# Fillers before the first scores, key maxima and block sums moved, two weight quarters moved, two weight differences on GpSimd

## The chip, the cores and the metric

One core of one Trainium2 chip runs the whole program. TensorE (PE) multiplies, VectorE (DVE), ScalarE (ACT) and GpSimd (POOL) work beside it, SyncE (SP) issues most of the transfers. The metric is the time of one execution on the device, in microseconds (us). A run of three executions before the change gave a median of 551.72 us.

## The reference

Three blocks follow each other. First comes attention for 2 batches, 8 heads and 768 positions of 64 values: every query sees the keys less than 16 positions away, and beside them one summary per block of 32 positions (the maximum of the keys, the mean of the values):

```
k_sum = k.reshape(B, H, nb, block, D).max(axis=3)
v_sum = v.reshape(B, H, nb, block, D).mean(axis=3)
scores_all = concat([where(|i-j| < 16, scale * q @ k.T, -1e9), scale * q @ k_sum.T + log(block)])
a = softmax(scores_all)
x = a @ concat([v, v_sum])
```

Then comes a mixture of eight experts over the 1536 tokens of 512 values. Each token goes to the expert with the largest logit, and is weighted with the softmax and a sigmoid gate:

```
e_idx = argmax(x @ w_gate)
out[t] = gate_w[t] * eom[t, e] * (relu(x[t] @ w1[e]) @ w2[e])
```

Last comes a gated projection, `(sigmoid(x @ w_gate) * (x @ w_val)) @ w_out`, with 1536 inner values.

## The kernel before

The large products are made of three products of parts: a value is split into a high part (written by ACT, `hi`) and the difference to it (`lo`, line 134, on DVE unless another engine is named), and high times high, high times low and low times high are summed in PSUM, the accumulators of TensorE.

**Attention** goes in 12 tiles of 128 queries (T = 0 to 5 the first batch, 6 to 11 the second). `s1` makes the scores of a tile in two halves: a mask (line 312), then four pairs of heads (line 316) against the keys and the key maxima, then a minimum of the (negated) scores on DVE (`nm`) and the exponentials on ACT. `s3` transposes the exponentials (line 344, copied as `aT` by ACT), `s4` multiplies them with the values (line 354), `s6` transposes the result to `xT` (line 370), `s7` makes the logits of the experts (line 379). The order over the tiles is written out in one loop over T; scores run ahead of the products by two tiles.

`ksum(b, p)` makes the maxima of the keys of batch b for the pair of heads p: five instructions on DVE, the last of which (line 255) writes them where `s1` reads them. `vsum_part` adds the values of blocks, for the second batch on GpSimd (lines 272 and 274). `place_sums(b)` transposes these sums with TensorE (line 286) and writes them into the value tiles `vt` (one half by DVE, the other by ACT at line 290, then copies on GpSimd at line 294). `keep_warm(n)` issues n matmuls whose result nobody uses (line 300, bf16, 128x512); eight of them run before the first mask. PSUM has banks by tags: A (3 banks), B (2), C (one tile of two banks, which also holds the result `xp` of `s4`) and M (1, for fillers, routing and single results).

**Experts.** `route` finds each token's expert and rank from the logits. `find_first` finds the tokens of the first item (an item is up to 256 tokens of one expert): `ff` is its generator, and `run(ff, n)` issues its next n stages. Its last stages are twelve small matmuls (line 608, which take `place`, written by DVE), two instructions on DVE and two gathers on GpSimd (line 613). `item_T` transposes the gathered tokens (line 642). `item_A(f)` is the f-th eighth of the first layer: twelve matmuls (line 653), then `hh` on ACT (line 655) and `hl` on DVE (line 656), which frees the bank of tag A. `item_B(f)` is the second layer. The weights are split by quarters: `split1(p)` for `w1`, `split2(p)` for `w2`, a high part by ACT and a difference by DVE (128x1024 each). There are seven items in the fixed part; the table of the items (`tb`, its tiles are named `o_...`) is worked out on DVE and GpSimd during the first and the second.

**The projection** follows, with its weights split in the same way (`wl` on GpSimd, `yb` on DVE).

Three sequences matter for the change: the first scores (lines 318 to 325), the loop over T (`ksum`, `place_sums` and `run(ff, 9)` stand at fixed T), and the stretch behind the loop (`item_A(0)`, `split1(1)`, `s6(11)`, `item_A(1)`, `run(p1, 1)`, `split1(2)`), with the loop over the items, where `split2(f // 2)` follows every even `item_A(f)`.

Of the kernel before, what the change touches and what calls it, by code (L numbers as in the profile page):

```python
# [10 lines left out]
F32 = mybir.dt.float32  # L11
# [22 lines left out]
C = 128  # L34
# [74 lines left out]
def moe_kernel(tc, A, out):  # L109
# [23 lines left out]
    def lo(o, i, h, eng=None):  # L133
        (eng or V).tensor_tensor(out=o, in0=i, in1=h.bitcast(F32), op=ALU.subtract)  # L134
# [145 lines left out]

    def place_sums(b):

        sp = ps.tile([128, 2, 512], F32, tag="C", bufs=1, name=f"sp{b}")[:, 0]
        for c in range(4):
            for p0 in (32, 96):
                PE.matmul(sp[p0:p0 + NB, c * 128:c * 128 + 128], vsum[b][:, c, 0:NB], ident, start=True, stop=True)
        heads = lambda x: x.rearrange("p (h x) -> p h x", h=H)
        first = vt[b, 0]
        ts(heads(first[32:32 + NB, 0, 1])[:, :, 0:D], heads(sp[32:32 + NB]), 1.0 / BLK, ALU.mult)
        SC.mul(heads(first[96:96 + NB, 0, 0])[:, :, 0:D], heads(sp[96:96 + NB]), 1.0 / BLK)  # L290
        for half in range(2):
            for par, p0 in ((0, 96), (1, 32)):
                n = 2 + half
                G.tensor_copy(vt[b, half][p0:p0 + NB, 3 - n:3, par], first[p0:p0 + NB, 0:1, par].to_broadcast([NB, n, VW]))

    def keep_warm(n):

        w = bank("M", 1)
        for _ in range(n):
            PE.matmul(w, warm[:, 0:128], warm, start=True, stop=True)  # L300

    def s1(T, halves=(0, 1)):

        b, m = divmod(T, TB)
        if ("a", T) not in st:
            st["a", T] = at.tile([128, 8, C], F32, tag="a", bufs=3, name=f"a{T}")
        a = st["a", T]
        sc = {half: bank("A", 3)[:, 0:4 * C].rearrange("p (g c) -> p g c", c=C) for half in halves}

        def mask(half):  # L310
            v = variant(2 * m + half)
            PE.matmul(sc[half], sel, mask4[:, v:v + 1].to_broadcast([67, 4, C]), start=True, stop=False)

        def score(half, pr):
            c0 = col_start(2 * m + half)
            PE.matmul(sc[half][:, pr], qz[T][:, pr, half], kg[b][:, pr, c0:c0 + C], start=False, stop=pr == 3)

        if T == 0:
            for half in halves:
                mask(half)  # L320
            for pr in range(4):
                for half in halves:
                    score(half, pr)
                if pr < 3:
                    keep_warm(4)
        for half in halves:
            if T:
                mask(half)
                for pr in range(4):
                    score(half, pr)  # L330
            scv = sc[half]
            nm = at.tile([128, 4], F32, tag="nm", bufs=4, name=f"nm{T}{half}")
            pace.append(red(nm, scv, ALU.min))
            for pr in range(4):
                SC.activation(out=a[:, half * 4 + pr], in_=scv[:, pr], func=AF.Exp, bias=nm[:, pr:pr + 1], scale=-1.0)
# [295 lines left out]
        hi(w1h[:, :, s], w1r[:, :, s])  # L631
        lo(w1l[:, :, s], w1r[:, :, s], w1h[:, :, s], eng)

    def split2(p):
        s = slice(2 * p, 2 * p + 2)
        hi(w2h[:, s], w2r[:, s])
        lo(w2l[:, s], w2r[:, s], w2h[:, s])

    def item_T(i, h, tag=("B", 2)):
        tp = bank(*tag).rearrange("p (g c) -> p g c", g=4)  # L640
        for c in range(4):
            PE.transpose(tp[:, c], xg[i % 2][:, h, c * 128:c * 128 + 128], ident)
        s = slice(h * 128, h * 128 + 128)
        hi(xTh[:, :, s], tp)
        lo(xTl[:, :, s], tp, xTh[:, :, s])
# [175 lines left out]
    def run(g, n=1):  # L821
        for _ in range(n):
            next(g, None)

    with tc.manual_schedule():
# [31 lines left out]
        for T in range(NT):  # L857
# [3 lines left out]
            if T < 2:  # L861
                for half in range(2):
                    s1(T + 1, (half,))
                    if T == 1 and half == 0:
                        place_sums(0)
                    s3(T, (half,))
                    if T == 0:
                        vsum_part(0, 2 + half)
                if T == 1:
                    spread_q(3)  # L870
            else:
                if T < NT - 1:
                    s3(T)
                if T == 3:
                    spread_q(5)
                if T == NT - 1:
                    item_T(0, 0, ("A", 3))
                    item_T(0, 1, ("A", 3))
                for t in q8:
                    s7(t)  # L880
                if T == NT - 2:
                    s3(T + 1)
                    split1(0)
                for t in now[:-1]:
                    s4(t)
                for t in first:
                    s1(t, (0,))
                if T == 8:
                    run(ff, 1)
                for t in q6:  # L890
                    s6(t)
                if T == 5:
                    place_sums(1)
                if 2 < T < NT - 3:
                    spread_q(T + 3)
                for t in first:
                    s1(t, (1,))
                if T == 2:
                    spread_q(4)
                if T == 3:  # L900
                    ksum(1, 1)
                if T == 8:
                    run(ff, 1)
                if T > 8:
                    run(g, 1)
            for t in now[-1:]:
                s4(t)
            if T == 8:
                run(ff, 9)
            for t in then:  # L910
                s1(t)
            for t in q7:
# [23 lines left out]
                    vsum_part(1, c)  # L936
            if T == 2:
                ksum(1, 0)
            if T == 3:
                ksum(1, 2)  # L940
                ksum(1, 3)
            if 2 < T < 7:
                load_q(T + 5)
            if T == 4:
                V.memset(low, 0.0)
                for e in range(1, 8):
                    V.memset(low[:, e, 0:e], 1.0)
# [34 lines left out]
        hl = mB.tile([128, 8, SLOT], F32R, name="hl")  # L982
        run(p1, 1)
        item_A(0)
        split1(1)
        s6(11)
        item_A(1)
        run(p1, 1)
        split1(2)
        item_gather(0, gidx[:, 16], S)  # L990
        item_gather(1, gidx[:, 17], S)
        item_A(2)
# [23 lines left out]
        for i in range(NSTAT):  # L1016
# [6 lines left out]
            if i:  # L1023
                for f in range(8):
                    item_A(f)
                    if f % 2 == 0:
                        split2(f // 2)
                    elif i > 1:
                        run(bg, 1)
                    if i == 1:  # L1030
                        if f in (1, 3, 4, 5):
                            run(tb, 1)
                        if f == 5:
                            for t in yrt:
                                G.memset(t, 0.0)
                            item_regs(2)
                            item_gather(2, gidx[:, 2])
# [221 lines left out]
```

## Time and profile before

| | |
|---|---|
| three executions | 551.72, 550.05, 551.89 us (median 551.72) |
| profiled execution | 552.54 us, of which its span is 550.7 us |
| PE busy | 535.8 us, 97% of the span |
| DVE, ACT, POOL busy | 388.1, 213.0 and 125.8 us (70, 39 and 23%) |

The span reaches from the first to the last record of the profile; 1.84 us of the execution lie outside it. Matmul ends are modelled, so that the rows below are best read by their starts. A row of the time line is: start, duration (of all its instructions, if it stands for several), engine, line, operation, result and operands, shape, number of instructions, and in brackets the idle time before it with what ended that.

### The profile page before, as it was taken

What the parts mean: (1) busy time and instruction counts of PE and PEld (TensorE: products, weight loads), DVE (VectorE), ACT (ScalarE), POOL (GpSimd) and SP (SyncE); (2) the same over time, 40 slices, a digit from 0 to 9 for tenths busy, and PEclk for the clock granted to TensorE, in tenths of its full rate; (3) what the DMA queues carried; (4) which work ended last, traced back from release to release, by engine and by line L of the source; (5) the groups of instructions that cost most, each with busy time, mean ns of one, the idle gap of its engine ahead of it and who ended that gap; (6) DMA issues with size and microseconds to landing.
All of it is one profiled execution on the core that took longest, in us unless ns stands there. A gap on an engine that the chain in (4) does not pass through costs nothing.

```text
span 550.7 us, 8924 instructions
## 1 busy us (share of the span) xinstructions
PE 535.8 (97%) x3236; PEld 456.5 (83%) x3236; DVE 388.1 (70%) x737; ACT 213.0 (39%) x390; POOL 125.8 (23%) x151
## 2 busy tenths in 40 slices
PE   8999989999999999999999999999999999999995
PEld 4788979888989989878888888888888888888884
DVE  4886768898778677853878899999998753323330
ACT  2786765755546455643221221211111442122110
POOL 3663145072101101000010111102101152212211
PEclk9999999999999999999999999999999999999998
DMA  8992368971568403216132323323322000001000
GB/s 326 411 412 88 132 231 273 335 277 39 183 244 280 160 6 119 70 57 211 39 114 78 114 80 112 115 83 109 114 76 77 1 2 38 20 38 39 21 37 39
DMA packets 31984, 71.63 MB, mean 130 GB/s; under 512 B 3056, under 2 KB 11712, under 8 KB 31936
## 3 DMA queue, kind: packets, MB, share of 16 engines
q1 hardware_dynamic: 28816, 60.96, 32.0%
q0 software_dynamic: 3120, 10.06, 5.5%
q8 instruction: 26, 0.43, 0.3%
q14 instruction: 22, 0.18, 0.1%
HBM read 72.53 MB, written 11.33 MB: 152 GB/s over the span
## 4 chain that ended last, share of the span: by engine, by line
PE 34%; issue 15%; POOL 5%; ACT 0%; POOLq 0%; DVE 0%; DVEq 0%; ACTq 0%
PE ps_A L1143 18%; PE ps_B L1143 15%; POOL out_dram L1191 3%; POOL yb L134 2%; PE ps_B L747 1%; POOLq L1255 0%; ACT yb L131 0%; ACT gs L131 0%; DVE gg L137 0%; POOLq L1191 0%; DVEq L137 0%; POOLq L134 0%; ACTq L131 0%
## 5 line engine op out<-in xcount | busy, mean ns | idle before, releaser
L1184 PE MATMUL ps_A<-yb,gs 128*128 128x512 f32 x432 | 98.1, 389 | 0.0
L1143 PE MATMUL ps_A<-yb,wh 128*128 128x512 f32 x312 | 96.8, 392 | 0.1
L1184 PEld LDWEIGHTS ps_A<-yb,gs 128*128 128x128 f32 x432 | 81.2, 188 | 16.8
L1143 PE MATMUL ps_B<-yb,wh 128*128 128x512 f32 x264 | 81.3, 390 | 0.0
L1143 PEld LDWEIGHTS ps_A<-yb,wh 128*128 128x128 f32 x312 | 57.9, 188 | 12.0 <-issue 0.6
L1143 PE MATMUL ps_A<-yb,wl 128*128 128x512 f32 x156 | 60.8, 390 | 0.0
L134 POOL TENSOR_TENSOR wl<-cvw,wh 128x512 fp32r<-128x512 f32 x20 | 26.7, 1334 | 137.7 <-ACT wh L131 137.7
L1143 PEld LDWEIGHTS ps_B<-yb,wh 128*128 128x128 f32 x264 | 49.6, 188 | 10.2
L1152 ACT ACTIVATE sg<-ps_A 128x512 f32<-128x512 f32 x36 | 21.4, 595 | 91.4 <-PE ps_A L1143 91.3
L653 PE MATMUL ps_A<-xTh,w1h 128*128 128x256 f32 x192 | 54.9, 286 | 1.0 <-DVE hl L656 1.0
L653 PE MATMUL ps_A<-xTh,w1l 128*128 128x256 f32 x192 | 54.5, 284 | 0.6 <-DVE w1l L134 0.6
L653 PE MATMUL ps_A<-xTl,w1h 128*128 128x256 f32 x192 | 54.4, 283 | 0.0
L1143 PE MATMUL ps_B<-yb,wl 128*128 128x512 f32 x132 | 51.4, 389 | 0.0
L131 ACT ACTIVATE gs<-gg 128x768 fp32r<-128x768 f32 x24 | 20.3, 846 | 69.6 <-PE ps_A L1184 67.4
L134 DVE TENSOR_TENSOR gs<-gg,gs 128x768 fp32r<-128x768 f32 x24 | 23.0, 958 | 34.2 <-ACT gs L131 34.1
L143 DVE TENSOR_SCALAR cva<-cva 128x512 f32<-128x512 f32 x72 | 43.3, 602 | 1.9
L134 DVE TENSOR_TENSOR w2l<-w2r,w2h 128x1024 fp32r<-128x1024 f32 x28 | 34.2, 1225 | 9.9 <-ACT w2h L131 9.1
L662 PE MATMUL yp<-w2h,hh 128*128 128x512 f32 x96 | 39.0, 407 | 0.0
L653 PEld LDWEIGHTS ps_A<-xTh,w1h 128*128 128x128 f32 x192 | 36.8, 192 | 1.6 <-DVE hl L656 1.4
L662 PE MATMUL yp<-w2h,hl 128*128 128x512 f32 x96 | 37.6, 392 | 0.0
L662 PE MATMUL yp<-w2l,hh 128*128 128x512 f32 x96 | 37.5, 391 | 0.0
L653 PEld LDWEIGHTS ps_A<-xTh,w1l 128*128 128x128 f32 x192 | 36.8, 192 | 0.8 <-DVE w1l L134 0.8
(232 smaller groups left out, 965.5 us busy)
## 6 DMA issues: line engine op xcount, KB each, us to landing
w1r<-in_w_dram SPq DMA_DIRECT2D x28, 512.0 KB
w2r<-in_w_dram SPq DMA_DIRECT2D x28, 512.0 KB
raw<-in_wgv_dram SPq DMA_DIRECT2D x24, 512.0 KB
vt<-in_vv_dram SPq DMA_DIRECT2D x12, 520.0 KB
raw<-in_wo_dram SPq DMA_DIRECT2D x12, 512.0 KB
kg<-in_kg_dram SPq DMA_DIRECT2D x8, 496.0 KB
y_c<-yt SPq DMA_DIRECT2D x13, 256.5 KB
yr<-y_c SPq DMA_DIRECT2D x12, 256.5 KB
```

What stands on the lines that cost most here:

```text
L131: SC.activation(out=o, in_=i, func=AF.Copy)
L134: (eng or V).tensor_tensor(out=o, in0=i, in1=h.bitcast(F32), op=ALU.subtract)
L143: V.tensor_scalar(out=o, in0=a, scalar1=s1, scalar2=s2, op0=op0, op1=op1)
L653: PE.matmul(hp, w[:, c, s], x[:, c], start=n == 0, stop=n == 11)
L662: PE.matmul(yp[h], x[:, f, s], w[:, f], start=f == 0 and n == 0, stop=f == 7 and n == 2)
L747: PE.transpose(tp[:, c], r[:, c * 128:c * 128 + 128], ident)
L1143: PE.matmul(pp, w[:, c], x[:, c], start=n == 0, stop=n == 11)
L1152: SC.activation(out=sg, in_=pp, func=AF.Sigmoid)
L1184: PE.matmul(po, g2[:, x, f % 6], yb[f // 4][w][:, f % 4], start=f == 0 and n == 0, stop=f == 11 and n == 2)
L1191: d = G.indirect_dma_start(out=out[:, :], out_offset=bass.IndirectOffsetOnAxis(ap=row_id[:, t:t + 1].bitcast(U32), axis=0), in_=ot, in_off ...
```

## The change

- In the first tile's scores, the fillers `keep_warm` stand before each of the four pairs of heads, 4, 3, 3 and 2 of them; before, 4 stood behind each of the first three pairs. Both make 12.
- `place_sums` takes the bank of tag M. Before, it took the tile of tag C.
- `ksum(1, 1)` moves from T = 3 to the end of T = 2, `ksum(1, 2)` from the end of T = 3 to the old place of `ksum(1, 1)`. `ksum(1, 3)` stays.
- `place_sums(1)` moves from the middle of T = 5 to the end of T = 4.
- `run(ff, 9)`, with the matmuls and the gathers of `find_first`, moves from the last third of T = 8 to T = 9, behind `s3(9)`.
- `split1(1)` moves from behind `item_A(0)` to T = 11, behind `item_T`; `split1(2)` from behind `run(p1, 1)` to the place ahead of it.
- `split2` takes an engine. For item 1, `split2(0)` and `split2(1)` make their differences on GpSimd.

```diff
     def place_sums(b):
-        sp = ps.tile([128, 2, 512], F32, tag="C", bufs=1, name=f"sp{b}")[:, 0]
+        sp = bank("M", 1)
...
         if T == 0:
             for half in halves:
                 mask(half)
-            for pr in range(4):
+            for pr, n in enumerate((4, 3, 3, 2)):
+                keep_warm(n)
                 for half in halves:
                     score(half, pr)
-                if pr < 3:
-                    keep_warm(4)
...
-    def split2(p):
+    def split2(p, eng=None):
         s = slice(2 * p, 2 * p + 2)
         hi(w2h[:, s], w2r[:, s])
-        lo(w2l[:, s], w2r[:, s], w2h[:, s])
+        lo(w2l[:, s], w2r[:, s], w2h[:, s], eng)
...
                 if T < NT - 1:
                     s3(T)
+                if T == 9:
+                    run(ff, 9)
...
                     item_T(0, 1, ("A", 3))
+                    split1(1)
...
-                if T == 5:
-                    place_sums(1)
...
                 if T == 3:
-                    ksum(1, 1)
+                    ksum(1, 2)
...
-            if T == 8:
-                run(ff, 9)
...
             if T == 2:
                 ksum(1, 0)
+                ksum(1, 1)
             if T == 3:
-                ksum(1, 2)
                 ksum(1, 3)
...
             if T == 4:
+                place_sums(1)
                 V.memset(low, 0.0)
...
         item_A(0)
-        split1(1)
         s6(11)
         item_A(1)
+        split1(2)
         run(p1, 1)
-        split1(2)
...
                     if f % 2 == 0:
-                        split2(f // 2)
+                        split2(f // 2, G if i == 1 and f < 4 else None)
```

On DVE, around the end of T = 2 (the `ks` and `kt` rows with line 255 behind them are one `ksum`, `nm` the minima of a half tile of scores, `xT` the copy behind `s6`). Before:

```order
L255 COPY kg_107<-ks_481 128x6x24
L146 TENSOR_REDUCE nm_510<-ps_A 128x4
L372 COPY xT_521<-ps_B 128x512
L146 TENSOR_REDUCE nm_531<-ps_A 128x4
L146 TENSOR_REDUCE ks_537<-kg_107 128x6x2
L146 TENSOR_REDUCE kt_538<-kg_107 128x12
L146 TENSOR_REDUCE ks_537<-kg_107 128x6
L137 TENSOR_TENSOR ks_537<-kt_538 128x6
L255 COPY kg_107<-ks_537 128x6x24
```

and after:

```order
L255 COPY kg_107<-ks_482 128x6x24
L146 TENSOR_REDUCE ks_489<-kg_107 128x6x2
L146 TENSOR_REDUCE kt_490<-kg_107 128x12
L146 TENSOR_REDUCE ks_489<-kg_107 128x6
L137 TENSOR_TENSOR ks_489<-kt_490 128x6
L255 COPY kg_107<-ks_489 128x6x24
L146 TENSOR_REDUCE nm_518<-ps_A 128x4
L371 COPY xT_529<-ps_B 128x512
L146 TENSOR_REDUCE nm_539<-ps_A 128x4
```

The second pair's maxima stand ahead of a tile's two minima where they stood behind them.

On POOL, in the second item (`o_es` belongs to the table of the items, `yt` to the output of the first item, `yr` are buffers of the projection). Before:

```order
L524 COPY o_es<-cs 128x8 x2
L707 COPY yt_1749<-xg_87 128x1
L707 COPY yt_1753<-xg_87 128x1
L1035 MEMSET yr_1639 128x520
L1035 MEMSET yr_1640 128x520
```

and after:

```order
L523 COPY o_es<-cs 128x8 x2
L706 COPY yt_1750<-xg_87 128x1
L706 COPY yt_1754<-xg_87 128x1
L134 TENSOR_TENSOR w2l<-w2r,w2h 128x1024 x2
L1033 MEMSET yr_1640 128x520
```

Two differences of 128x1024 stand between the output's copies and the buffers' memsets.

On DVE, in the first four eighths of the second item (`hl` ends an eighth, `o_le`, `o_lf` and `o_tf` are the table's). Before:

```order
L656 SCALAR_TENSOR_TENSOR hl<-ps_A,hh 128x256
L134 TENSOR_TENSOR w2l<-w2r,w2h 128x1024
L656 SCALAR_TENSOR_TENSOR hl<-ps_A,hh 128x256
L137 TENSOR_TENSOR o_le<-o_cc,ck 128x104 x2
L137 TENSOR_TENSOR o_le<-o_le 128x104
L137 TENSOR_TENSOR o_lf<-o_le,o_es 128x728
L656 SCALAR_TENSOR_TENSOR hl<-ps_A,hh 128x256
L134 TENSOR_TENSOR w2l<-w2r,w2h 128x1024
L656 SCALAR_TENSOR_TENSOR hl<-ps_A,hh 128x256
```

and after:

```order
L655 SCALAR_TENSOR_TENSOR hl<-ps_A,hh 128x256 x2
L137 TENSOR_TENSOR o_le<-o_cc,ck 128x104 x2
L137 TENSOR_TENSOR o_le<-o_le 128x104
L137 TENSOR_TENSOR o_lf<-o_le,o_es 128x728
L655 SCALAR_TENSOR_TENSOR hl<-ps_A,hh 128x256 x2
```

The two `w2l` are gone from DVE; the table's four instructions stand between the second and the third `hl` as before.

## Rows read from the trace of the kernel before

**Rows 1.** Time line of TensorE, the first scores.

```profile
7.03 1.20 PE L316 MATMUL ps_A<-kg,qz 128*128 128x128 f32 x4 [0.30 <-ACT qz L239]
8.02 1.92 PE L300 MATMUL ps_M<-w2r 128*128 128x512 bf16 x4
9.73 1.06 PE L316 MATMUL ps_A<-kg,qz 128*128 128x128 f32 x4
...
11.99 0.61 PE L316 MATMUL ps_A<-kg,qz 128*128 128x128 f32 x4
12.44 1.03 PE L300 MATMUL ps_M<-w2r 128*128 128x512 bf16 x4
13.30 0.61 PE L316 MATMUL ps_A<-kg,qz 128*128 128x128 f32 x4
```

**Rows 2.** Time line of DVE in the same stretch.

```profile
10.87 0.23 DVE L255 COPY kg<-ks 128x144 f32<-128x144 f32 x1
13.72 1.29 DVE L146 TENSOR_REDUCE nm<-ps_A 128x4 f32<-128x512 f32 x2 [2.62 <-PE ps_A L316]
```

**Rows 3.** Time line of all engines, keys and block sums of the second batch.

```profile
41.89 0.49 PE L316 MATMUL ps_A<-kg,qz 128*128 128x128 f32 x2 [0.79 <-DVE kg L255]
...
43.17 0.23 POOL L274 TENSOR_TENSOR vs<-w1r 128x24 f32<-128x24 f32 x1
...
48.84 1.06 PE L286 MATMUL sp<-ident,vs 128*24 128x128 f32 x16
...
51.42 1.16 PE L354 MATMUL xp<-vt,aT 128*64 128x65 f32 x32 [0.31 <-ACT vt L290]
```

**Rows 4.** Time line of TensorE and POOL, tokens of the first item and its first layer.

```profile
71.18 0.84 PE L608 MATMUL ps_M<-ckb,place 128*128 128x2 bf16 x9 [0.38 <-DVE place L143]
...
75.34 1.00 POOL L613 DMA_INDIRECT xg<-x_t,gix  x1 [0.31 <-issue]
...
83.53 1.09 PE L642 MATMUL ps_A<-ident,xg 128*128 128x128 f32 x8
...
92.25 0.39 PE L653 MATMUL ps_A<-xTh,w1l 128*128 128x256 f32 x1 [0.62 <-DVE w1l L134]
```

**Rows 5.** Time line of POOL, DVE and TensorE, first eighths of the second item.

```profile
118.81 1.34 POOL L707 COPY yt<-xg 128x1 int32<-128x1 int32 x2
...
120.36 0.43 DVE L137 TENSOR_TENSOR o_le<-o_cc,ck 128x104 f32<-128x104 f32 x2
...
120.83 0.27 DVE L137 TENSOR_TENSOR o_le<-o_le 128x104 f32<-128x104 f32 x1
...
121.19 0.92 DVE L137 TENSOR_TENSOR o_lf<-o_le,o_es 128x728 f32<-128x728 f32 x1
...
121.92 0.28 PE L653 MATMUL ps_A<-xTh,w1l 128*128 128x256 f32 x1
122.03 0.42 DVE L656 SCALAR_TENSOR_TENSOR hl<-ps_A,hh 128x256 fp32r<-128x256 f32 x1
...
122.50 0.39 PE L653 MATMUL ps_A<-xTh,w1h 128*128 128x256 f32 x1 [0.30 <-DVE hl L656]
```

**Rows 6.** Differences on GpSimd, a group of the page: total, mean ns, idle before.

```profile
L134 POOL TENSOR_TENSOR wl<-cvw,wh 128x512 fp32r<-128x512 f32 x20 | 26.7, 1334 | 137.7 <-ACT wh L131 137.7
```

**Rows 7.** Time line of DVE and POOL, differences on both engines.

```profile
438.21 2.38 DVE L134 TENSOR_TENSOR yb<-wo,yb 128x512 fp32r<-128x512 f32 x2
...
438.42 5.13 POOL L134 TENSOR_TENSOR yb<-wo,yb 128x512 fp32r<-128x512 f32 x3 [18.40 <-ACT yb L131]
...
441.72 0.68 DVE L134 TENSOR_TENSOR yb<-wo,yb 128x512 fp32r<-128x512 f32 x1
```

**Rows 8.** Stretches at the end: busy time of each engine, granted clock, DMA.

```profile
544.00:546.00 2.00, 0.36 (x2) 0.00 (x0) 0.46 (x1) 0.34 (x1) 0.49 (x1) 1.00 0.00 0
546.00:547.00 1.00, 0.00 (x0) 0.00 (x0) 0.00 (x0) 0.00 (x0) 0.48 (x1) 1.00 0.00 0
547.00:548.00 1.00, 0.00 (x0) 0.00 (x0) 0.00 (x0) 0.00 (x0) 0.00 (x0) 0.79 0.68 262
```

## The prediction, before the change was run

> **What bounds the kernel now.** I read the page first: TensorE is busy for 97% of the span (the table above), so that only its waits can be won, and its work at the slow rate. Then I went through TensorE's time line for starts that have an idle time in brackets. They add up to some 6 us, and nearly all stand before 126 us: from there until its last matmul, 0.36 into the stretch from 544 [rows 8], TensorE hardly waits (0.27 at 238 and 0.15 at 246), and the chain of work that ended last is its own matmuls. So what is won before 126 us moves the end by the same amount, and what is lost there does so too. Last I read, for each step that the change moves, the time line of the engine that releases TensorE there, and looked for other work of that engine in the new place.
>
> A term is the idle time of a row. The ends of matmuls are modelled, so such an idle time is short by a little: in the second item one product starts at 121.92 and the next at 122.50 [rows 5], 0.58 apart, while products of this kind follow each other by 0.12. That is a loss of 0.46 where the bracket says 0.30. I add 0.15 to each of the four waits that go and are read from a bracket, 0.6 in all.
>
> **The start.** Before, TensorE has a hole of 0.30 ahead of the first scores, which wait for `qz`. The first four fillers are spaced (9.73 - 8.02) / 4 = 0.43 apart, the last four (13.30 - 12.44) / 4 = 0.215 [rows 1]: these are the two levels of the clock, 1.2 and 2.4 GHz, and the rate rose a little before 11.99, some 11.7. The scores end at 13.7, when DVE's minima, idle for 2.62, begin [rows 2]. The change keeps the twelve fillers, and puts four of them where the hole is, and three ahead of the next pair. What it can give lies between two ends. If the rate rises at 11.7 as before, 0.3 of the hole is won and 0.1 in the order: 0.4. If it rises as the scores begin, the work left is 12 x 0.215 for fillers and 4 x 0.45 for pairs (12.44 - 11.99) [rows 1], 4.4 us from 6.7 on, or 11.1. But the fourth pair needs its maxima, which DVE ends at 10.87 + 0.23 = 11.10 [rows 2]. Its matmuls then end at 11.55, 2.2 before the old end. I take 2.1, since the row that the change touches is the hole, and behind the hole the rate rose while TensorE had no other; this is the weakest of my choices, and 0.4 stays as a rival.
>
> The Trainium skill ("TensorE: Matmul & The Clock Gate", Part 1) says that the moment at which the clock rises is not tied to the kernel's start and shifts from run to run, and advises against fitting to it. By that rule some executions would give 0.4 and some 2.2, and the median could lie anywhere between.
>
> **Key maxima.** `ksum(1, 1)` now stands before two minima of scores instead of behind them, so that its result, and that of `ksum(1, 2)`, are ready long before use. The wait of 0.79 at 41.89 [rows 3] goes. What is late next is the minima that stand behind it, and with them the exponentials on ACT. No row shows that; five small instructions take about as long as two minima, 1.3 [rows 2], and scores run two tiles ahead of their products. I take 0.1, within 0 and 0.7.
>
> **Block sums.** `place_sums(1)` leaves the place at 48.84 and goes to about 43 to 46. The wait of 0.31 for ACT's write into `vt` [rows 3] goes, since a whole step of scores then lies between. Does GpSimd deliver its last sum in time? It ends at 43.17 + 0.23 = 43.40 [rows 3], and TensorE, 3 us earlier here by the terms so far, reaches the sums at about 42.9 to 43.1. It first does three of the four columns (three quarters of 1.06, 0.8), so it reaches the last at 43.8: covered by 0.4. If that cover fails, it costs 0.4. The bank of tag M instead of C frees the tile of `xp`. ACT's write now stands ahead of a copy `aT` for the next tile: 0.1.
>
> **First tokens.** The wait of 0.38 for `place` at 71.18 [rows 4] goes, since in the next tile DVE has long written it. The price is in the gathers: they start one tile later. The second was issued at 75.34 and is behind one scatter now; `item_T` took the tokens at 83.53 [rows 4]. With the tile's shift of about 2 us on POOL they land at 81.5 to 82.1 by my count, and `item_T` comes at 83.0 at the earliest: covered by about 0.9. If not, TensorE waits for the excess.
>
> **Weight quarters.** The 0.62 at 92.25 is a wait for DVE's difference of the second quarter of `w1` [rows 4]. Two quarters are now begun earlier, so it goes. An ACT instruction of 128x1024 now stands ahead of the copy `xT` of the last tile but one: 0.1.
>
> Sum of gains: 2.1 + 0.79 + 0.31 + 0.38 + 0.62 + 0.6 = 4.8; less 0.3 for the small costs, 4.5.
>
> **The differences on GpSimd.** In the second item `hl` on DVE frees TensorE's bank, and the wait of 0.46 before 122.50 stands because DVE is late with it. Moving two `w2l` off DVE would remove it, if DVE's other work ran at its old speed. But the rows say something else. A difference of 128x512 takes GpSimd 1.334 [rows 6], so one of 128x1024 takes about 2.6. And when both engines work on differences, neither runs: DVE's two took 2.38 from 438.21 instead of 2 x 0.68, while GpSimd's three took 5.13 from 438.42 instead of 3 x 1.33 [rows 7]; together from 438.21 to 443.55, 5.34, which is the sum of all five, 1.36 + 4.0 = 5.4. They take turns, and each waits for the end of the other's instruction. GpSimd's copies of 118.81 were also held for 1.34 [rows 5]. Now see what DVE has at that time: `o_le` (0.43 for two, and 0.27) and `o_lf` (0.92) [rows 5], all of them with two operands in SBUF, and they stand between the second and the third `hl`. GpSimd begins when the copies are done, about 119.25, and has 5.2 us of work. If they take turns, DVE does one of its four in between, and is through with the others after both: 119.25 + 5.2 + 0.43 + 0.27 + 0.92 + 0.42 = 126.5 for the third `hl`, where it was 122.45. TensorE has three banks of tag A and stands from about 122 on. The loss is 126.4 - 122.5 = 3.9, in which the 0.46 is counted. Bounds: nothing (then 0.46 is gained), 1.3 (DVE keeps its turn after the first of the two), and 3.9. I take 3.9, because the rows in which both worked show turns.
>
> **Net:** 3.9 - 4.5 = -0.6. The profiled execution of 552.54 would become 551.9; it lies 0.8 above the median of the three, 551.72. On that median the forecast is **551.2**, with an own range of 549.6 to 552.8 (GpSimd's loss 1 lower, small costs up to 0.7, start 1 less).
>
> **Rivals.**
> - *GpSimd's differences stay hidden.* DVE's four instructions run beside them at their old speed, or DVE keeps its turn. Against it speak [rows 7]; for it, that the table's instructions are small. Gain 4.5 + 0.46 = 5.0: 546.7; with a loss of 1.3 it is 548.5.
> - *The wait slows the clock* (the slower side). The place is the third `hl` of the second item, the price is paid after it: TensorE stands for about 4 us. If the clock falls, work follows at half rate as at the start, where 4.7 us (7.03 to 11.7) [rows 1] passed at the low level, half of it lost: +2.3, so 553.5. Whether it falls depends on how long TensorE stands. At the end it stood from 544.4 [rows 8], and the granted clock was still 1.00 in 546 to 547 and 0.79 in 547 to 548 [rows 8]: it fell after some 3 us. With a longer stand than that the rival decides.
>
>   The Trainium skill (same page, "HAM oscillation") describes kernels whose waits throttle the clock again and again, with the cost of the start paid each time. By it the item would pay once more; the rows at the end speak for that.
> - *The start gives 0.4.* The rate rises when it did; the other terms stay: 552.9.
> - *The gathers are late.* TensorE reaches `item_T` before they land, by 1 to 2: 552.2 to 553.2. Against it, the cover of 0.9; for it, that this cover is a count over one moved scatter.
>
> **How the numbers follow.** The main case has 0.38, hidden differences 0.22 (half of it at 546.7, half at 548.5), the slower clock 0.20, the start 0.12, the gathers 0.08. Predicted is the time of the likeliest, 551.2. The range takes in the hidden case and the clock: 546.6 to 554.4. About 0.5%, 2.8 us, is what a measurement of this kernel can tell from no change, so faster means under 548.96 and slower over 554.48. Faster is the hidden case and a little of the main one: 0.24. Slower is the upper part of the clock's case, with a start that gives little: 0.13. The rest is same, 0.63.
>
> **What would show it.** Start: the first minima of DVE at about 11.6 instead of 13.72, and all of the last fillers spaced 0.215. Keys, sums, tokens and quarters: no idle bracket at the five places of before. Gathers: no wait ahead of line 642. Item: a `w2l` row of POOL with two instructions beside `o_le` and `o_lf` rows on DVE that are stretched to more than 2 each, and a line 653 that waits 3 to 4 us for `hl`; if the rows of DVE keep 0.43, 0.27 and 0.92, the main case is wrong. Clock: the granted clock of the stretch behind that wait, 1.00 or less.

## The result

The changed kernel takes 557.15 us (median of six executions, 555.92 to 558.74), the kernel before beside it 551.81; the ratio is 1.0099, with a 95% interval of 1.0073 to 1.0125. The forecast was 551.2, in a range from 546.6 to 554.4. The change costs 5.3 us where a gain of 0.6 was expected, and the time lies outside the range.

The profiled execution took 557.63 us, with a span of 555.8. Its page says less than one would think: TensorE is as busy as before.

```profile
PE 538.2 (97%) x3236; PEld 458.5 (82%) x3236; DVE 388.8 (70%) x735; ACT 213.1 (38%) x390; POOL 131.0 (24%) x153
...
PEclk9999989997999999999999999999999999999999
```

Here the second line is the granted clock of TensorE in 40 slices. It has two slices under 9, one that ends at 83 us and one from 125 to 139 us. Where the time went is read from the starts of the same matmuls in both traces. The next rows are the time line of TensorE in the changed kernel.

```profile
12.00 0.71 PE L316 MATMUL ps_A<-kg,qz 128*128 128x128 f32 x4 [0.18 <-DVE kg L255]
...
49.42 1.16 PE L353 MATMUL xp<-vt,aT 128*64 128x65 f32 x32
...
78.96 1.53 PE L343 MATMUL ps_B<-ident,a 128*128 128x128 f32 x8 [2.28 <-ACT aT L344]
...
81.45 1.85 PE L353 MATMUL xp<-vt,aT 128*64 128x65 f32 x32
83.23 1.09 PE L641 MATMUL ps_A<-ident,xg 128*128 128x128 f32 x8
...
91.26 0.28 PE L652 MATMUL ps_A<-xTh,w1l 128*128 128x256 f32 x1
...
95.53 0.39 PE L652 MATMUL ps_A<-xTh,w1h 128*128 128x256 f32 x1 [0.59 <-DVE hl L655]
...
121.61 0.28 PE L652 MATMUL ps_A<-xTh,w1l 128*128 128x256 f32 x1
125.39 0.58 PE L652 MATMUL ps_A<-xTh,w1h 128*128 128x256 f32 x1 [3.50 <-DVE hl L655]
```

Against the rows of before these make a ledger (after minus before, a minus is a gain):

| place | before | after | shift |
|---|---|---|---|
| last pair of the first scores [rows 1] | 13.30 | 12.00 | -1.3 |
| product behind the block sums [rows 3] | 51.42 | 49.42 | -2.0 |
| transposes of the first item's tokens [rows 4] | 83.53 | 83.23 | -0.3 |
| product that waited for the second quarter [rows 4] | 92.25 | 91.26 | -1.0 |
| last product ahead of the third `hl` [rows 5] | 121.92 | 121.61 | -0.3 |
| product behind it [rows 5] | 122.50 | 125.39 | +2.9 |
| span | 550.7 | 555.8 | +5.1 |

Three pieces are lost: 1.7 and more between 51 and 83 us, 3.2 in the wait for `hl`, and 2.2 behind that wait, where nothing waits. The clock explains the third, and a part of the first. These are stretches of the changed kernel, with the granted clock in the third column from the end:

```profile
80.00:82.00 2.00, 2.00 (x17) 1.36 (x17) 1.82 (x3) 0.75 (x2) 1.66 (x2) 0.50 0.23 60
82.00:84.00 2.00, 2.00 (x35) 1.93 (x32) 0.52 (x2) 0.28 (x2) 0.98 (x1) 0.75 0.91 331
...
122.00:125.00 3.00, 0.00 (x0) 0.00 (x0) 2.86 (x4) 1.26 (x2) 3.00 (x5) 0.83 0.00 0
125.00:127.00 2.00, 1.61 (x7) 1.61 (x8) 2.00 (x6) 0.00 (x0) 0.44 (x1) 0.50 0.00 0
127.00:130.00 3.00, 3.00 (x16) 3.00 (x15) 2.76 (x13) 0.38 (x1) 0.00 (x0) 0.50 0.00 0
130.00:132.00 2.00, 2.00 (x16) 2.00 (x15) 0.97 (x4) 1.08 (x2) 0.61 (x1) 0.81 0.00 0
```

Behind the stand of 2.28 us TensorE runs at 1.2 GHz from 80 to about 83 us: the 32 products at 81.45 take 1.85 where they took 1.16 at 49.42. Behind the wait of 3.50 it does so from about 124 to 131 us, and the shift grows from 2.9 to 5.2 there.

### The profile page after: what moved, and what is told of

Same layout as the page of the kernel before. It is cut to its first block, busy times and chain, and to the rows that moved or that the text cites. A ratio compares the mean times of both kernels' runs of the same rounds, so it can differ in the third digit from the quotient of the medians.

```text
span 555.8 us, 8924 instructions
## 1 busy us (share of the span) xinstructions
PE 538.2 (97%) x3236; PEld 458.5 (82%) x3236; DVE 388.8 (70%) x735; ACT 213.1 (38%) x390; POOL 131.0 (24%) x153
## 4 chain that ended last, share of the span: by engine, by line
PE 34%; issue 14%; POOL 5%; ACT 0%; POOLq 0%; DVE 0%; DVEq 0%; ACTq 0%
PE ps_A L1141 18%; PE ps_B L1141 15%; POOL out_dram L1189 3%; POOL yb L134 2%; PE ps_B L746 1%; POOLq L1253 0%; ACT yb L131 0%; ACT gs L131 0%; DVE gg L137 0%; POOLq L1189 0%; DVEq L137 0%; POOLq L134 0%; ACTq L131 0%
## 5 line engine op out<-in xcount | busy, mean ns | idle before, releaser
L652 PEld LDWEIGHTS ps_A<-xTh,w1h 128*128 128x128 f32 x192 | 38.0, 198 | 5.6 <-DVE hl L655 5.4
L134 DVE TENSOR_TENSOR w2l<-w2r,w2h 128x1024 fp32r<-128x1024 f32 x26 | 31.8, 1227 | 10.4 <-ACT w2h L131 9.6
L652 PEld LDWEIGHTS ps_A<-xTl,w1h 128*128 128x128 f32 x192 | 38.0, 198 | 0.2
L1189 POOL DMA_INDIRECT out_dram<-yr,row_id x12 | 19.2, 1602 | 78.3 <-DVE yr L1185 70.9
```

Source lines behind the costliest of these rows:

```text
L652: PE.matmul(hp, w[:, c, s], x[:, c], start=n == 0, stop=n == 11)
L1189: d = G.indirect_dma_start(out=out[:, :], out_offset=bass.IndirectOffsetOnAxis(ap=row_id[:, t:t + 1].bitcast(U32), axis=0), in_=ot, in_off ...
```

## The experiments

Kernels were timed in groups, each beside the kernel before on one chip (where an expectation says "call", it means such a group). The ratio is to the kernel before of the same group, with a 95% interval.

### Where the loss in the second item comes from

**The differences back on DVE.** The changed kernel with one edit undone:

```diff
-                        split2(f // 2, G if i == 1 and f < 4 else None)
+                        split2(f // 2)
```

> The changed kernel with the second item's two weight differences back on DVE, all else as changed. Theory: the two differences on GpSimd hold DVE's table instructions (turns), TensorE stands 3.5 us, and the clock falls behind it; together the shift between the traces goes from -0.3 to +5.2 us there. Then this kernel takes back about 5.5: 551.6 us, and the granted clock behind 122 us stays at 1.00. Rival: only the stand of TensorE comes from GpSimd, the clock falls there anyway, since the changed kernel already fell once at 80 us: 553.8, with 0.5 in the clock of 122 to 130 us.

Measured: 552.61 us, ratio 1.0015 (1.0005 to 1.0025). The time lies between the theory's 551.6 and the rival's 553.8. On the clock the theory holds: it falls at 80 us and is 1.00 from 122 to 130 us. So this part carries 4.6 of the loss, most of what was expected; the other edits together cost 0.9, though they were to gain 4.5.

**The differences alone.** The kernel before with that line alone.

> The kernel before with nothing but the second item's two differences on GpSimd. Theory: turns (3.2) plus the clock's fall (2.3) cost the same without the other edits: 551.8 + 5.5 = 557.3 us, o_le on DVE stretched to over 4 us for two, granted clock 0.5 behind the wait. Rival: the clock falls only together with the fall at 80 us, so that here the stand alone counts: 555.0. If DVE is not held, 551.3.

Measured: 556.39 us, ratio 1.0099 (1.0081 to 1.0117): 4.7 slower, less than the 5.5 of the theory and more than the 3.2 of the rival. The time line of POOL and DVE in the changed kernel shows how:

```profile
118.80 4.75 POOL L134 TENSOR_TENSOR w2l<-w2r,w2h 128x1024 fp32r<-128x1024 f32 x2
...
118.95 4.73 DVE L137 TENSOR_TENSOR o_le<-o_cc,ck 128x104 f32<-128x104 f32 x2
123.71 0.27 DVE L137 TENSOR_TENSOR o_le<-o_le 128x104 f32<-128x104 f32 x1
124.08 0.92 DVE L137 TENSOR_TENSOR o_lf<-o_le,o_es 128x728 f32<-128x728 f32 x1
124.92 0.75 DVE L655 SCALAR_TENSOR_TENSOR hl<-ps_A,hh 128x256 fp32r<-128x256 f32 x2
```

Two `o_le` that took 0.43 [rows 5] take 4.73, one for each difference on POOL. They begin with POOL and end with POOL (123.55 and 123.68), and what follows has its old durations. With the part alone the two take 4.71, so it needs none of the other edits.

The Trainium skill ("SBUF — State Buffer", Who interferes with whom) states that a DVE instruction with two inputs in SBUF contends with a GpSimd instruction that reads SBUF, and calls the hold on the ports that they share an exclusive lock. The rows agree: `o_le` has two such inputs, and each waits for one difference of 2.4 us.

**The wait filled.** The kernel before with the differences on GpSimd, and 16 matmuls (`keep_busy`, bf16 128x512 into the bank of tag M, from `xTh`) ahead of the sixth eighth:

```diff
                 for f in range(8):
+                    if i == 1 and f == 5:
+                        keep_busy(16)
                     item_A(f)
```

> As the kernel before with the two differences on GpSimd, and 16 matmuls of bf16 128x512 (results unused) ahead of the sixth eighth of the second item, so that TensorE works through most of the time in which it would stand (16 x 0.215 = 3.4 us). Theory: the wait stays, the clock's fall goes: 2.3 less than without the fillers, 555.0 us, granted clock 1.00 through 120 to 132. Rival: the loss behind the wait has another source (DVE late in its later work): the fillers change nothing, 557.3 us.

Measured: 554.80 us, ratio 1.0064 (1.0045 to 1.0082), 1.6 less than without them. The time line of TensorE shows that they fill the wait, and the stretch behind has the full clock:

```profile
121.05 3.63 PE L307 MATMUL ps_M<-xTh 128*128 128x512 bf16 x16
124.71 0.39 PE L660 MATMUL ps_A<-xTh,w1h 128*128 128x256 f32 x1
```

```profile
125.00:127.00 2.00, 2.00 (x19) 2.00 (x19) 2.00 (x3) 0.38 (x1) 0.00 (x0) 1.00 0.00 0
```

The mean granted clock over the six executions is 0.9968 with the fillers and 0.9935 without; in the kernel before beside them it is 0.9962. A stretch of t us at the low level lowers the mean of a span by 0.5 t over the span, and loses t/2 of work, so the difference of 0.0033 is worth 0.0033 x 553 = 1.8 us. That is what the times differ by. So the part costs 3.1 by the wait and 1.6 by the clock on average; the intervals of the two ratios just meet (1.0081 and 1.0082), so that the 1.6 is known roughly. Not every execution pays the second piece. The profiled one of the kernel with the differences alone stood for 3.48 us and kept its clock, while it fell once at 72 to 76 us, with TensorE busy throughout:

```profile
72.00:74.00 2.00, 2.00 (x11) 1.92 (x11) 0.86 (x7) 0.75 (x2) 1.55 (x2) 0.52 0.89 296
74.00:76.00 2.00, 2.00 (x12) 1.85 (x11) 0.69 (x1) 1.05 (x5) 1.68 (x2) 0.63 1.04 355
...
122.00:125.00 3.00, 0.02 (x1) 0.02 (x1) 2.86 (x5) 0.87 (x1) 3.00 (x5) 1.00 0.00 0
125.00:127.00 2.00, 2.00 (x17) 2.00 (x18) 2.00 (x4) 0.29 (x1) 0.03 (x1) 1.00 0.00 0
```

The Trainium skill ("TensorE: Matmul & The Clock Gate", HAM oscillation) describes kernels in which waits of TensorE throttle it and the cost of the start is paid again. The means agree, the single execution shows that such a wait doesn't always do it.

### Where the gain in the attention went

**The tokens back in T = 8.** The changed kernel with `run(ff, 9)` in its old place.

> The changed kernel with the matmuls and gathers of the first item's tokens back in T = 8. Theory: the stand of 2.28 us at 76.7 us comes from the gathers' place one tile later, and the clock's fall at 80 us from that stand; back in T = 8 the stand is about 1.1 as before and the clock stays: 2.5 won, 0.65 lost for the wait on place, so 555.3 us. Rival: the stand ends at a fixed time, when the first gather has landed, whatever TensorE does before; TensorE, 2 us earlier than in the kernel before, then stands over 2 us here too and the clock falls: 557 us.

Measured: 556.28 us, ratio 1.0078 (1.0058 to 1.0099). The stand is 1.06 instead of 2.28, but the clock fell behind it all the same. About 1 is won (0.9 by the two medians, 0.0021 by the ratios); that lies between the theory's 1.8 and the rival's nothing, and the two intervals overlap, so that the time alone doesn't tell it from nothing. What shows the edit's part is the length of the stand.

**Single parts on the kernel before.** The fillers alone, the key maxima with the block sums, and the two quarters of `w1`, each as in the change's diff:

> The kernel before with nothing but the fillers of the first scores moved (4, 3, 3, 2 ahead of the pairs). Theory: the scores end 1.2 us earlier, as in the changed kernel, but the sums of blocks then wait longer for GpSimd at 18 us (0.9 instead of 0.5), so 0.8 is kept: 550.9 us. Rival: the moment at which the clock rises varies from one execution to the next in the kernel before as well, and the order of the fillers gives nothing on the median: 551.7.

Measured: 549.94 us against 550.04, ratio 0.9995 (0.998 to 1.001). The fillers give nothing that can be told from zero.

> The kernel before with the key maxima moved, and the block sums moved and in bank M. Theory: the waits of 0.79 and 0.31 go, with what the brackets leave out 1.2: 550.5 us, no bracket ahead of the score matmuls at 40 us and ahead of line 354 at 50 us. Rival: what is won here is given back in the stand near 79 us, if its end hangs on the gather's data and not on TensorE: then the stand there grows from 1.1 to 2.3 and the time is 551.6.

Measured: 549.53, ratio 0.9990 (0.9978 to 1.0002). The brackets are gone, and products stand where the theory has them:

```profile
41.07 1.05 PE L316 MATMUL ps_A<-kg,qz 128*128 128x128 f32 x8
...
49.40 1.15 PE L354 MATMUL xp<-vt,aT 128*64 128x65 f32 x32
```

The time shows 0.5 of the 1.2, with an interval that reaches from a gain of 1.2 to nothing. In the profiled execution the granted clock fell to 0.75 and 0.65 in 70 to 76 us, with no wait there.

> The kernel before with nothing but the two quarters of w1 moved. Theory: the wait of 0.62 at 92 us goes (0.8 with what the bracket leaves out), and a new one of 0.6 stands four matmul groups later, for hl, which now queues on DVE behind the difference of the third quarter: net 0.1, 551.6 us. Rival: the new wait comes from the other edits (TensorE earlier against DVE), and here the whole 0.8 is won: 550.9.

Measured: 550.34, ratio 1.0010 (1.0001 to 1.0020). The 0.62 at 92 us is gone and a wait of 0.58 for `hl` stands at 93.7, as in the changed kernel. The theory holds: no gain.

**The kept parts.** Fillers, key maxima, block sums and the second quarter only.

> The kernel before with the fillers, the key maxima, the block sums and the second quarter of w1 moved; left as before are the tokens of the first item, the third quarter and the differences on DVE. Theory: 0.8 + 1.2 + 0.8 add up, and without the longer stand at 79 us and the stand at 122 us the clock stays: 548.9 us, which beats both kernels. Rival: the stand near 79 us swallows what was won ahead of it: 550.9.

Measured: 548.58 us, ratio 0.9981 (0.9968 to 0.9995): faster than the kernel before and, by the ratios, than the changed one. With the third quarter in its old place there is no bracket between 79 and 113 us.

**The tokens alone, and with the kept parts.**

> The kernel before with nothing but the matmuls and gathers of the first item's tokens moved to T = 9. Theory: the wait on place goes (0.65), TensorE then stands 2.3 us at 77 to 79 instead of up to 1.1, and in most executions the clock falls behind that: 1.2 to 2.3 more for the stand and some 1 for the clock, so 1.5 to 2.5 slower than the kernel before. Rival: the stand of 2.3 comes from TensorE being 2 us earlier there by the other edits; alone this edit gives 0.65 and costs nothing: 0.6 faster than before.

Measured: 549.44, ratio 0.9979 (0.9966 to 0.9991). The theory falls here: alone, and with no stand in its profile, the edit gains 0.85.

> The kept parts (fillers, key maxima, block sums, second quarter) with the tokens of the first item in T = 9 as well. Theory: 1.5 to 2.5 slower than the kept parts alone, a stand of 2.3 us at 75 to 78 and a lower mean clock. Rival: 0.6 faster than the kept parts.

Measured: 548.10, ratio 0.9953 (0.9937 to 0.9969), the fastest of the kernels that gather the right tokens. The theory falls here too. No stand is seen:

```profile
77.57 1.07 PE L344 MATMUL ps_B<-ident,a 128*128 128x128 f32 x8
```

This is the time line of the kernel with the tokens alone; where the changed kernel has its bracket of 2.28, there is none.

**The stand filled, and plain loads.** Two kernels that were to explain the stand, in a group in which it didn't occur. The first has ten fillers of the same kind, the second loads in place of the gathers:

```diff
                 if T == NT - 2:
+                    keep_busy(10)
                     s3(T + 1)
```

> The kept parts with the tokens in T = 9, and ten matmuls of bf16 128x512 (results unused) ahead of the last tile's transposes, where TensorE stands (10 x 0.215 = 2.15 us). Theory: the stand stays, since its end does not hang on TensorE, and the clock no longer falls behind it: faster than the same kernel without these fillers by what its clock loses, about 1 us, mean clock 0.997. Rival: the clock has no part in it; the fillers give nothing or cost their own time, up to 2.

Measured: 550.56, ratio 0.9997 (0.9987 to 1.0008), 2.5 slower than without these fillers: there was nothing to fill, and they cost their own 2.15.

> The kept parts with the tokens in T = 9, the two gathers by token list on GpSimd replaced by two plain loads of the first 256 rows on SP (the rows are then not the item's tokens). Theory: the stand at 77 us comes from the gathers' transfers, which run through GpSimd's queue; without them it is gone or under 0.5, and the clock stays: as fast as the kept parts or 0.6 faster. Rival: the stand comes from the scatters or the load of w1 that run at the same time, and stays at 2.3.

Measured: 547.93, ratio 0.9950 (0.9934 to 0.9966), within 0.2 of the kernel with the gathers. Since that one had no stand here either, this says nothing about the stand's cause.

**The same kernels once more, together.** The changed kernel, the one with the differences on DVE, the kept parts with the tokens, and the kernel before.

> The changed kernel once more, beside the next three on one chip. Open is whether its stand of 2.3 us near 77 us belongs to the program or to the conditions of the chip at that time: the kernel before, the one without GpSimd's differences and three others had a stand there when they were profiled beside each other, and none of the eight kernels profiled later had one. Theory (conditions): all kernels of this call agree; where no stand is seen, the changed kernel costs the differences' 4.7, the third quarter's 0.65, and wins 2.2: 3.1 slower than the kernel before. Where the stands are back, 5.4 slower. Rival (program): 5.4 slower with the stand, whatever the others show.

Measured: 558.36, ratio 1.0121 (1.0096 to 1.0145).

> The changed kernel with the differences back on DVE, once more. Theory (conditions): without stands in this call it is 1.5 faster than the kernel before; with them 0.9 slower. Rival (program): 0.9 slower and a stand of 2.3 us, though the next kernel, which has the third quarter in its old place and is the same up to 90 us, shows none.

Measured: 552.67, ratio 1.0018 (1.0001 to 1.0035).

> Kept parts and tokens in T = 9, once more. Theory (conditions): without stands 2.2 faster than the kernel before, as in its first run; with them, a stand of 2.3 us and 0.2 slower than the kernel before. Rival (program): 2.2 faster, no stand, also where the other two show one.

Measured: 553.10, ratio 1.0013 (0.9996 to 1.0029). The same code had 0.9953 before.

> The kernel before, profiled here. Theory (conditions): without stands no idle bracket of 1.07 near 79 us, and about 1 us less than in the call in which the changed kernel was timed (550.3 against 551.7); with them the bracket of 1.07 and 551.7. Rival (program): the bracket of 1.07 in either case.

Measured: 552.58 here; 550.04 and 550.29 were the medians of the kernel before in the two groups ahead of this one. The time lines of the four, in this order, at the transposes behind the logits:

```profile
79.77 1.54 PE L343 MATMUL ps_B<-ident,a 128*128 128x128 f32 x6 [1.97 <-ACT aT L344]
```

```profile
79.08 1.52 PE L343 MATMUL ps_B<-ident,a 128*128 128x128 f32 x8 [2.08 <-ACT aT L344]
```

```profile
80.03 1.14 PE L343 MATMUL ps_B<-ident,a 128*128 128x128 f32 x8 [2.00 <-ACT aT L344]
```

```profile
80.03 1.15 PE L344 MATMUL ps_B<-ident,a 128*128 128x128 f32 x8 [0.57 <-ACT aT L345]
```

All four stand in the one execution that was profiled. The times say the same of the whole group: none of the twelve executions of the kept parts with the tokens was under 550.54 us, where none of six had been over 548.53 before. So the stand belongs to conditions that a whole group shares, and not to the place of the third quarter, nor to one chip: the group of e1 to e4 and that of e9 to e12 ran on the same chip. In the groups with stands (this one and the first, with e1 to e4) the kernels with the tokens in T = 9 stand for 2.0 to 2.3, those with T = 8 for 0.6 to 1.1; one profile there has none, that of the differences alone, in which TensorE came late by the clock's fall at 72 to 76 us. In the groups without it, none of ten profiled kernels stands.

**The kept parts again, with and without the fillers.**

> The kept parts (fillers, key maxima, block sums, second quarter of w1) once more, with the tokens in T = 8 as in the kernel before. Theory (the stand near 78 us depends on conditions and is longer with the tokens in T = 9): where stands are seen in this call, the stand is 1.1 at most here and the gains of about 1.5 stay, mean ratio to the kernel before 0.997; where none is seen, 0.998 as in its first run. Rival: where stands are seen, they swallow the gains, 1.000, as for the kept parts with the tokens in T = 9.

> The kept parts without the fillers' new order. Theory: the fillers' order gives nothing on the median, since the clock rises as early in most executions of the kernel before: the same time as with them, within 0.4 us. Rival: they give the 0.8 us that the two first traces show between them: 0.8 slower than with them.

Measured: 548.64, ratio 0.9978 (0.9962 to 0.9993), and 548.77, ratio 0.9977 (0.9966 to 0.9987). There were no stands in this group, so the kept parts were not seen beside one. The fillers give nothing: the theory holds.

## Why the prediction was wrong

**The differences on GpSimd: the mechanism was right, its size near.** The prediction had turns, the third `hl` at 126.5 and a loss of 3.9. Measured were an `hl` that ends at about 125.3 and a loss of 3.2 (2.9 + 0.3). A difference takes 2.38 instead of the 2.6 worked out from the 128x512 row, and DVE got its turns beside the two differences. The turns were read from [rows 7] with a slip: five differences are added up there, but DVE's third (0.68 at 441.72) lies in the same 5.34 us, and the six alone would take 6.0. The engines do take turns there, at a little less than the sum.

**The clock: the price was near, its chance was wrong.** The rival "the wait slows the clock" had 2.3 us; 2.3 is what the shift grows by in the changed kernel, 1.6 the average over executions. The step that failed is the chance of 0.20. The prediction's own working had TensorE stand for about 4 us and the clock fall after some 3 us at the end [rows 8], "with a longer stand than that the rival decides". By that it was the likeliest case. The rivals were also priced one at a time: the clock and a start that gives 0.4 can come together, and by the prediction's own prices that is 551.2 + 2.3 + 1.7 = 555.2, above the range.

**The start: the step that failed is the one row.** The term of 2.1 was read from an execution that is unlike most. Its minima begin at 13.72 [rows 2]; in later profiles of the kept parts with the old order of the fillers (first) and with the new one (second) they begin together:

```profile
12.65 1.29 DVE L146 TENSOR_REDUCE nm<-ps_A 128x4 f32<-128x512 f32 x2 [0.58 <-PE ps_A L316]
```

```profile
12.54 1.29 DVE L146 TENSOR_REDUCE nm<-ps_A 128x4 f32<-128x512 f32 x2 [0.58 <-PE ps_A L316]
```

In both the last pair starts within 0.2 of the end of the fourth key maxima, at 12.07 and 11.95. The prediction named that bound, at 11.10, but not that the old order comes as near to it, nor that the bound itself moves: in the changed kernel it is 11.94, since the second part of the keys was late (DVE took it up at 7.85, before at 7.03). The rival "the start gives 0.4" was nearest.

By the Trainium skill ("TensorE: Matmul & The Clock Gate", Part 1) the moment of the rise varies from run to run. These profiles agree: in the first of the two above, the four fillers behind the first pair take 1.03 from 7.54 us, at the high level already, where they took 1.92 from 8.02 us [rows 1]. That late rise made the term of 2.1.

A part of what the start won in the trace went to a second limit. The sums of blocks waited 0.52 for DVE before; in the changed kernel, 1.3 earlier, they waited 0.89 for GpSimd.

**Key maxima and block sums: right, but the second is worth less.** The brackets of both went. Between the products ahead of and behind each place the shift grows by 1.0 for the keys and by 0.1 for the sums, where 0.84 and 0.36 were counted (the brackets with 0.15 each, less 0.1 each). The cover for GpSimd's last sum held. The wait for exponentials that was named as the next one (0.1, within 0 and 0.7) isn't in the first profile of the changed kernel; it stands at 36 to 37 us in four of the thirteen profiles with the key maxima moved, with 0.23 to 0.73.

**First tokens: half right.** The wait for `place` went, worth 0.65, and the gathers were in time for `item_T`: no bracket stands ahead of line 641. What failed is that the prediction put at nothing, without a reason, what the edit does to a wait of the kernel before. This is the row; its cause is not known:

```profile
80.42 1.15 PE L344 MATMUL ps_B<-ident,a 128*128 128x128 f32 x8 [1.07 <-ACT aT L345]
```

The wait of 1.07 stands some 3 us behind the gathers that were moved. In the changed kernel it is 2.28, and the clock's fall behind it costs 1.2 more (shift from -1.46 at 78.96 to -0.30 at 83.23). An unexplained wait beside an edit is an unknown price, and it should have widened the range on the slower side.

**Weight quarters: what is late next was not named.** The 0.62 went, and the product at 91.26 is 0.7 further ahead than the one at 83.23. But at 95.53 TensorE waits 0.59 for `hl`. These are DVE's rows of before (the product it frees started at 95.87, without a wait), and then of after:

```profile
94.92 0.42 DVE L656 SCALAR_TENSOR_TENSOR hl<-ps_A,hh 128x256 fp32r<-128x256 f32 x1
```

```profile
95.06 0.41 DVE L655 SCALAR_TENSOR_TENSOR hl<-ps_A,hh 128x256 fp32r<-128x256 f32 x1
```

That `hl` did not move, though TensorE came earlier. On DVE the third quarter's difference now stands ahead of ten small instructions of the table of the items, and they stand ahead of this `hl`. It waits for ACT's high part, and they with it:

```profile
92.58 1.23 DVE L134 TENSOR_TENSOR w1l<-w1r,w1h 128x1024 fp32r<-128x1024 f32 x1 [0.52 <-ACT w1h L131]
```

With the third quarter left in place there is no such wait. So the second quarter's move gains and the third's gives it back.

**Summed up for the changed kernel, in groups with stands:** the differences cost 4.7, the longer stand and the clock behind it some 2, and the third quarter about 0.65; won are 1.2 by keys and sums, 0.65 by the tokens and 0.8 by the second quarter (0.62 in its row and 0.15 to 0.2 beside it). That makes 4.7; measured were 5.3 and 6.1. In groups without stands the changed kernel was not run; by the parts it would be about 3 slower, which is only argued. Against the forecast 5.9 are missing (557.15 - 551.2): the start's 2.1, the clock's 1.6, some 2 by the stand and the clock behind it, and the third quarter's 0.65, less 0.8 by which the wait for GpSimd (3.1) was shorter than the 3.9. That makes about 5.6. The stand and the third quarter had no term in the prediction.

**What stays open** is the cause of the stand. TensorE's products there have started and end by the trace, and DVE and ACT begin on them late. As the ends are modelled, the trace does not tell whether the products were held or only their signals. GpSimd gives a lead: it issues gathers and scatters there, four behind each other, and in each of the nine profiles with a stand DVE goes on 0.6 to 0.9 us after the last of the four ends. In the changed kernel it ends at 77.70, in the kernel before in the last but one group at 78.48, where the product of line 354 had started at 75.86 with 1.15 to do:

```profile
76.67 1.03 POOL L442 DMA_INDIRECT x_s<-w2r,posi  x1 [0.30 <-issue]
78.27 0.17 DVE L141 TENSOR_SCALAR rs<-xp 128x8 f32<-128x8 f32 x1 [3.69 <-remote]
```

```profile
77.48 1.00 POOL L443 DMA_INDIRECT x_s<-w2r,posi  x1 [0.30 <-issue]
79.33 0.17 DVE L141 TENSOR_SCALAR rs<-xp 128x8 f32<-128x8 f32 x1 [2.60 <-PE ps_B L344]
```

With the tokens in T = 9 the four end later against TensorE's work (3.9 us behind the start of that product in the changed kernel, 2.6 in the kernel before), which fits the longer stand. They are not enough by themselves: most profiles without a stand have the same instructions, and DVE goes on while they run. So a link is suggested, and not shown.

Which conditions decide, no run here tells: the kernel with plain loads fell into a group without stands. It is open, too, whether the kept parts keep their gain beside a stand; the fastest kernel lost its 2.2 there.

## What to carry to other kernels

Before work of DVE is put on GpSimd, list what DVE still has at that time: here each of two small instructions with two inputs in SBUF waited for one of GpSimd's, 2.4 us each. A new wait of TensorE of several microseconds is priced with the clock's fall behind it, and rivals that can come together are added before the range is drawn. A term that rests on one execution's start is checked against a second limit before it is counted, and an unexplained wait next to an edit belongs in the range.

## What the runs showed of the hardware

- One program has times that differ by the group: the kernel before had medians of 550.0, 550.3 and 550.3 us in the groups without stands, 551.7 and 552.2 in those with them. It isn't the clock alone: its executions with a mean granted clock of 0.996 or more have medians of 549.9 to 550.2 in the former, 551.3 and 551.4 in the latter. In the group with 552.2 its executions range from 550.45 us at a mean granted clock of 0.998 to 554.46 at 0.993.
- The granted clock fell to 0.52 and 0.63 in 72 to 76 us in an execution of the differences alone in which TensorE was busy for the whole of those stretches; its last wait before was one of 0.38 at 69.50.
- Fillers in a wait of TensorE of about 3.5 us brought back some 1.6 us of 4.7, although they do no useful work.
